# Attention with a soft mixture of experts: the last weights by column halves for two experts in place of three, the first output by halves for eighteen tokens a row in place of fifteen

## The chip, the cores and the metric

The kernel runs on one core of a Trainium2 chip. The metric is the device time of one execution in microseconds (us), the median of several. Beside it there is one profiled execution, with its own time and its span: the span runs from the first to the last instruction of the trace, the time also covers what lies around them.

## The reference

Sliding-window attention (8 batches, 8 heads, 576 positions, head size 64, window 64) makes the 4608 x 512 matrix x. A soft mixture of 8 experts with 4 slots each follows:

```python
def _moe_ref(x, phi, w1, w2):
    logits = x @ phi                                  # 4608 x 32
    d = softmax of logits over the tokens
    slot_input = (d.T @ x).reshape(8, 4, 512)
    for e in range(8):
        h = np.maximum(slot_input[e] @ w1[e], 0.0)    # 512 -> 1024
        slot_out[e] = h @ w2[e]                       # 1024 -> 512
    c = softmax of logits over the slots
    return c @ slot_out                               # 4608 x 512
```

Inputs and output are 32-bit floats. The slots' input needs the softmax over all tokens, so the experts come after the whole attention; the output needs the slots' result of all experts, so no row of it can be written before the last expert's weights are in.

## The kernel before

**Attention.** 32 steps (pairs of heads) run through a pipeline written out by hand: transposes of k and q, row maxima, scores, exponentials, products with v, and in between the logits, the running softmax over the tokens and the sum for the slots' input. q, k, v and the weights are loaded by GpSimd, whose transfers turn 32-bit floats into 16-bit ones on the way. All of these loads stand in one queue, in the order in which GpSimd issues them. There are eight semaphores for them, used in turn, so an issue waits until the transfer eight places before it has landed; what stands behind it on GpSimd waits too.

**Weights.** `w1_t[e]` and `w2_t[e]` hold the first and second matrices of the experts. Those of experts 0 to 6 have room of their own. `load_w(i)` (L136) loads a whole one, 1 MB in 16 bit: i = 0 to 6 are first matrices, i = 7 to 13 second ones, so that i = 12 is the second matrix of expert 5. In the loop over the steps twelve of them are issued (i = 0 to 11). Expert 7's matrices take over buffers of the staged k and q: `load_last1` (L146) loads a quarter of its first matrix, `load_half` (L154) a piece of its second.

`load_half(i)` loads a quarter of the second matrix of an expert, 256 KB: rows of one half (h) and columns of one half (d). Before the change it counts through experts 5, 6 and 7, first for the left 256 columns (i = 0 to 5), then for the right ones (i = 6 to 11). Eight of these are issued at L733, when the last staged rows have gone, the other four in the expert phase, between the `cb_sub` (L532), which GpSimd also computes.

**Experts.** `first` (L859) and `turn_hidden` (L874) make the hidden values, all experts of a group of four at once, in parts of the array. `second_first` (L881) multiplies with the second matrices of experts 0 to 3, over all columns. `second(d)` (L887) does it for experts 4 and 5 in column half d, `second_last(d)` (L893) for experts 6 and 7. Sums are gathered in `ops[d]`; a copy by ScalarE turns that into `osb`, the right side of the last product, each column half by itself (L967, L979).

**Output.** A row of the output is taken from the softmax over the slots: `ct4[k]` holds it, transposed, for 1152 tokens (k = 0 to 3), nine per partition, made by `spread` (two batches each); `sums(k)` makes the reciprocals of its sums. `give(k, e0, ne, c0, nc_)` (L940) computes `ne` of the nine tokens of each partition, from column c0 on, `nc_` columns wide: a matmul per token into `cp`, an eviction that scales it by the reciprocal, by turns on ScalarE (L957) and VectorE (L955), and one transfer to memory by SyncE (L959). A piece of ne tokens has, for each partition, ne runs of 1 KB if it is half the columns wide, and one run of ne x 2 KB if it is whole, since the nine tokens of a partition follow one another in memory. The pieces take seven buffers in turn (`obs`, the place of first matrices that are no longer used), so that an eviction of a piece waits for the transfer seven pieces before it.

The engines' queues run in the order of the program text: on TensorE `second(0)`, `second_last(0)`, left halves of k = 0, `second(1)`, left halves of k = 1, `second_last(1)`, right halves, and the rest with both halves together.

Of the kernel before, what the change touches and what calls it, by code (L numbers as in the profile page):

```python
# [18 lines left out]
def kernel(  # L19
# [12 lines left out]
    B, H, S, Dh = q.shape  # L32
# [97 lines left out]
    def w1_dram(e):  # L130
        return moe_w1[e].rearrange("(p c) f -> p c f", c=NKK)

    def w2_dram(e):
        return moe_w2[e].rearrange("(h p c) d -> p h c d", h=2, c=NFC // 2)

    def load_w(i):  # L136
        second, e = divmod(i, NRES)
        if second:
            nc.gpsimd.dma_start(out=w2_t[e, 0][:, :, :].rearrange("p (h c) d -> p h c d", h=2), in_=w2_dram(e))
        else:  # L140
            nc.gpsimd.dma_start(out=w1_t[e, 0], in_=w1_dram(e))

    last = E - 1
# [8 lines left out]
    DH = D // 2  # L152

    def load_half(i):  # L154
        d, i = divmod(i, 6)
        e, h = last - 2 + i // 2, i % 2
        if e == last:
            if h == 0:
                w2_t[last].append([])
            c = pin.tile([128, 4, DH], FP16, name="w2h", tag="ks")  # L160
            w2_t[last][d].extend(c[:, j, :] for j in range(4))
        else:
            c = w2_t[e, 0][:, 4 * h:4 * h + 4, DH * d:DH * d + DH]
        nc.gpsimd.dma_start(out=c, in_=w2_dram(e)[:, h, :, DH * d:DH * d + DH])

    def w2_at(e, d, fc):
        return w2_t[e][d][fc] if e == last else w2_t[e][fc][:, DH * d:DH * d + DH]
# [362 lines left out]
    def cb_sub(b, eng):  # L530
        lgT = lgs[b]
        eng.tensor_tensor(out=lgT[:, :, :], in0=lgT[:, :, :],  # L532
                          in1=cbs[b][:, :].unsqueeze(2).broadcast_to([128, 6, 32]), op=ALU.subtract)
# [7 lines left out]
    def cb_turn(b):  # L541
        nc.vector.transpose(ct_all[:, b, :], cbs.pop(b)[:, :, :].rearrange("p i s -> p (i s)"))
# [144 lines left out]
    NE = 2 * S // 128  # L687
# [12 lines left out]
    def spread(b, copy, rp=None):  # L700
        if rp is None:
            rp = psr.tile([128, 1024], FP32, name="rp", tag="rp")
        for t in range(5):
            w = 128 if t < 4 else 64
            nc.tensor.matmul(rp[:, 128 * t:128 * t + w], ss4[:, min(t, 3), :],
                             ct_all[:, b, 128 * (t // 4):128 * (t // 4) + w], start=True, stop=True,
                             skip_group_check=True)
        copy(out=ct4[b // 2][:, :, 64 * (b % 2):64 * (b % 2) + 64],
             in_=rp[:, 0:S].rearrange("p (x e) -> p e x", e=NE))
# [7 lines left out]
    def sums(k):  # L717
        rp = psr.tile([128, 1024], FP32, name="rp", tag="rp")
        for e in range(NE):
            nc.tensor.matmul(rp[:, e:e + 1], ct4[k][:, e, :], one[:, :], start=True, stop=True, skip_group_check=True)  # L720
        nc.vector.reciprocal(rcs[:, k, :], rp[:, 0:NE])  # L721
# [8 lines left out]
    load_last1()  # L730
    make_ss4()
    nc.gpsimd.tensor_copy(out=ssf, in_=ss)
    for i in range(8):  # L733
        load_half(i)
    st_score8(p - 3)
    st_exp8(p - 3)
# [122 lines left out]
    def first(g, f2):  # L859
        ha, _ = bank("ha")  # L860
        for kk in range(NKK):
            for j in range(4):
                nc.tensor.matmul(ha[32 * j:32 * j + 32, :], sit[:, kk, :],
                                 w1_t[4 * g + j][kk][:, 512 * f2:512 * f2 + 512],
                                 start=(kk == 0), stop=(kk == NKK - 1), skip_group_check=True)

        hv = ha[:, :].rearrange("p (x c) -> p c x", c=4)
        if f2 == 0:
            nc.scalar.activation(hs_[:, g, f2], hv, AF.Relu, scale=emask[:, g:g + 1])
        else:  # L870
            nc.vector.tensor_scalar(out=hs_[:, g, f2], in0=hv, scalar1=emask[:, g:g + 1],
                                    scalar2=0.0, op0=ALU.mult, op1=ALU.max)
# [21 lines left out]
    def second_last(d):  # L894
        for j in (2, 3):
            for fc in range(NFC):
                i = fc % 4
                nc.tensor.matmul(ops[d][32 * i:32 * i + 32, :], hT[1][:, fc, 32 * j:32 * j + 32],
                                 w2_at(4 + j, d, fc), start=False, stop=(j == 3 and fc >= 4), skip_group_check=True)
# [3 lines left out]
    fr_turn(b)  # L903
    cb_max(b - 2)
    cb_sub(b - 2, nc.gpsimd)
    load_half(8)
    cb_turn(b - 3)
    first(0, 1)
    spread(1, act)
    cb_max(b - 1)  # L910
    cb_sub(b - 1, nc.gpsimd)
    load_half(9)
    first(1, 0)
    turn_hidden(0)
    sums(0)
    cb_exp(b - 2)
    cb_max(b)
    cb_sub(b, nc.gpsimd)
    load_half(10)
    load_half(11)  # L920
    first(1, 1)
    second_first(range(4))
    turn_hidden(1)
# [16 lines left out]
    def give(k, e0, ne, c0, nc_):  # L940
        nonlocal turn, piece
        ov = out[2 * S * k:2 * S * k + 2 * S, :].rearrange("(p e) d -> p e d", e=NE)
        ob = obs[piece % NRES][:, 0:ne * nc_].rearrange("p (e d) -> p e d", d=nc_)
        piece += 1
        n1 = 512 // nc_
        for i0 in range(0, ne, n1):
            n_ = min(n1, ne - i0)
            cp = pst.tile([128, n1, nc_], FP32, name="cp", tag="cp")
            for i in range(n_):
                nc.tensor.matmul(cp[:, i, :], ct4[k][:, e0 + i0 + i, :], osb[:, c0:c0 + nc_],  # L950
                                 start=True, stop=True, skip_group_check=True)
            for i in range(n_):
                rc = rcs[:, k, e0 + i0 + i:e0 + i0 + i + 1]
                if turn % 2:
                    nc.vector.tensor_scalar(out=ob[:, i0 + i, :], in0=cp[:, i, :], scalar1=rc, scalar2=None, op0=ALU.mult)  # L955
                else:
                    nc.scalar.activation(ob[:, i0 + i, :], cp[:, i, :], AF.Copy, scale=rc)  # L957
            turn += 1
        nc.sync.dma_start(out=ov[:, e0:e0 + ne, c0:c0 + nc_], in_=ob)  # L959
# [15 lines left out]
    sums(1)  # L975
    give(1, 0, 3, 0, DH)
    give(1, 3, 3, 0, DH)
    second_last(1)
    act(out=osb[:, DH:D], in_=ops[1])  # L979
    give(0, 0, 2, DH, DH)  # L980
# [3 lines left out]
    give(1, 0, 3, DH, DH)  # L984
    spread(5, dve)
    give(1, 3, 3, DH, DH)
    for k in range(1, B // 2):
        for e0 in range(6 if k == 1 else 0, NE, 3):
            give(k, e0, 3, 0, D)
            if k == 1:  # L990
                sums(2)
            if k == 2:
                if e0 < 6:
                    spread(6 + e0 // 3, (act, dve)[turn % 2])
                else:
                    sums(3)
# [28 lines left out]
```

## Time and profile before

| what | us or share |
|---|---|
| median of 3 executions | 192.83 (192.33 to 192.84) |
| the profiled execution, its time | 192.84 |
| its span | 191.1 |
| TensorE busy (matmuls) | 159.7 (84%) |
| VectorE busy | 143.6 (75%) |
| ScalarE busy | 129.6 (68%) |
| GpSimd busy | 108.2 (57%) |
| bytes moved by the DMA engines | 41.46 MB, 9.44 MB of it output |
| first and last output transfer issued | 158.6 and 181.9 |

The page gives, besides, a strip of 40 slices for each engine, with the DMA engines' busy share in tenths and the bytes moved, the chain of work that ended last, and the issues of transfers with their sizes. The trace has, for each transfer, its issue and its landing, and for each of the sixteen DMA engines the moment at which that engine's part has landed. Transfers of the loads are counted with their 16-bit bytes; twice as many are read from memory.

### The profile page before, as it was taken

How to read it: one execution, taken by the hardware profiler on the slowest of the kernel's cores; microseconds unless marked ns; L12 is line 12 of the kernel's file. 1: busy time of each engine (PE TensorE's matmuls, PEld its weight loads, DVE VectorE, ACT ScalarE, POOL GpSimd, SP SyncE). 2: the span in 40 equal slices, each digit the busy share in tenths (PEclk: the TensorE clock that was granted, in tenths of full speed). 3: DMA queues.
4: the chain of work that ended last, by engine and by line, in shares of the span. 5: the costliest groups of instructions: out<-in, count | busy, mean ns of one | idle time of the engine just before them, and what ended most of it. 6: DMA issues, size and time to landing. Idle time of an engine off the chain costs nothing. (4 is left out here: it accounts for less than half of the span.)

```text
span 191.1 us, 6805 instructions
## 1 busy us (share of the span) xinstructions
PE 159.7 (84%) x2887; PEld 115.8 (61%) x2887; DVE 143.6 (75%) x354; ACT 129.6 (68%) x249; POOL 108.2 (57%) x181
## 2 busy tenths in 40 slices
PE   7976989989999999998999999889889967189700
PEld 2555878876876877787687687757634544054200
DVE  5888788888888898899889889889864618058900
ACT  5576787887787787789788778875863525068700
POOL 7956876966869487598668748540935830000000
PEclk9999999999999999999999999999999999658975
DMA  6999999999999999999999999999999999959996
GB/s 164 216 188 182 187 189 219 175 222 180 185 225 177 219 182 185 224 178 215 188 186 213 187 206 196 212 203 205 212 209 200 198 194 234 292 196 356 408 417 253
DMA packets 64798, 41.46 MB, mean 217 GB/s; under 512 B 38912, under 2 KB 61184, under 8 KB 63872
## 3 DMA queue, kind: packets, MB, share of 16 engines
q0 software_dynamic: 58400, 30.35, 116.4%
q1 hardware_dynamic: 6368, 10.68, 16.0%
q8 instruction: 22, 0.36, 0.7%
q14 instruction: 8, 0.07, 0.1%
HBM read 61.93 MB, written 9.44 MB: 374 GB/s over the span
## 5 line engine op out<-in xcount | busy, mean ns | idle before, releaser
L391 DVE TENSOR_REDUCE m<-a_m 128x8 f16<-128x1024 f32 x32 | 39.1, 1220 | 0.0
L425 ACT ACTIVATE pt<-a_s 128x1024 f16<-128x1024 f32 x32 | 32.8, 1024 | 7.8 <-PE a_s L418 7.6
L359 POOL COPY qb<-qp 64x288 int32<-64x288 int32 x54 | 22.8, 423 | 23.3 <-ACT qp L356 19.9
L477 ACT COPY xt<-a_k 128x576 f16<-128x576 f16 x28 | 17.9, 638 | 12.7 <-PE a_k L473 12.7
L459 DVE TENSOR_TENSOR x_b<-a_v,rc 128x640 f16<-128x640 f32 x31 | 25.6, 824 | 1.1
L955 DVE TENSOR_SCALAR w<-cp,rcs 128x256 f32<-128x256 f32 (+1 forms) x25 | 13.5, 585 | 12.0 <-PE cp L950 11.3
L351 ACT ACTIVATE kT<-a_k 128x576 f16<-128x576 f16 x31 | 20.3, 655 | 1.0 <-PE a_k L340 1.0
L405 DVE TENSOR_TENSOR rt<-a_v,kind 36x256 f16<-36x256 f32 x30 | 12.8, 428 | 9.9 <-PE a_v L404 9.3
L180 POOL DMA_DIRECT2D v<-in_v_dram x16 | 20.1, 1254 | 0.0
L386 PE MATMUL a_m<-kT,qb 128*128 128x128 f16 x256 | 19.8, 220 | 0.0
L412 PEld LDWEIGHTS <-kT 128*128 128x128 f16 x288 | 18.6, 98 | 1.8 <-issue 1.4
L412 PE MATMUL a_s<-qb,kT 128*128 128x128 f16 x256 | 19.6, 219 | 0.0
L418 PE MATMUL a_s<-rt,lh 128*128 128x256 f16 x128 | 19.2, 273 | 0.4 <-DVE rt L405 0.4
L356 ACT ACTIVATE qp<-a_q 128x576 f16<-128x576 f16 x27 | 18.0, 668 | 1.7 <-PE a_q L340 1.7
L386 PEld LDWEIGHTS <-qb 128*128 128x128 f16 x256 | 14.6, 98 | 7.3 <-issue 5.4
L190 POOL COPY v<-v 64x576 int32<-64x576 int32 x16 | 10.6, 662 | 14.1 <-DMA v<-in_v_dram 13.6
L340 PE MATMUL a_q<-ident_h,qs 96*64 96x96 f16 x384 | 15.2, 207 | 2.8 <-DVE a_q L237 1.5
L449 PE MATMUL a_v<-v,pt 128*64 128x65 f16 x558 | 15.1, 195 | 0.6 <-DVE rt L405 0.4
L957 ACT ACTIVATE w<-cp,rcs 128x256 f32<-128x256 f32 (+1 forms) x26 | 12.7, 564 | 4.1 <-PE cp L950 2.5
L340 PEld LDWEIGHTS <-qs 96*64 96x64 f16 x384 | 12.5, 110 | 4.7 <-issue 4.4
L340 PE MATMUL a_k<-ident_h,ks 96*64 96x96 f16 x384 | 14.5, 212 | 0.1
L950 PE MATMUL cp<-qb,v 128*128 128x256 f16 (+1 forms) x51 | 12.7, 368 | 2.1 <-ACT w L957 1.1
(194 smaller groups left out, 351.0 us busy)
## 6 DMA issues: line engine op xcount, KB each, us to landing
w<-in_moe_w_dram POOLq DMA_DIRECT2D x12, 1024.0 KB, 15.9
out_dram<-w SPq DMA_DIRECT2D x7, 768.0 KB, 5.8
v<-in_v_dram POOLq DMA_DIRECT2D x16, 288.0 KB, 12.8
ks<-in_k_dram POOLq DMA_DIRECT2D x15, 288.0 KB, 13.6
qs<-in_q_dram POOLq DMA_DIRECT2D x15, 288.0 KB, 12.2
w<-in_moe_w_dram POOLq DMA_DIRECT2D x8, 256.0 KB, 10.4
out_dram<-w SPq DMA_DIRECT2D x5, 384.0 KB, 3.3
w1h<-in_moe_w_dram POOLq DMA_DIRECT2D x4, 256.0 KB, 16.3
```

The lines of the kernel that those rows point to most:

```text
L180: nc.gpsimd.dma_start(out=v1s[b % 2][:, c, 0:Dh], in_=v[b].rearrange("h s d -> (h s) d").rearrange("(c p) d -> p c d", p=128)[:, c, :])
L340: nc.tensor.transpose(tq[64 * hf:64 * hf + 64, RP * r:RP * r + RP], src[0:RP, h + hf, Dh * r:Dh * r + Dh], ident_h[0:RP, 0:RP])
L351: nc.scalar.activation(kTs[p % NK][:, 64:64 + S], turned(a_kh), AF.Copy, scale=QKS)
L356: nc.scalar.activation(qp, turned(a_qh), AF.Copy, scale=QKS)
L359: nc.gpsimd.tensor_copy(out=qbs[p % NQ][:, :, :, :].rearrange("p i l x -> p (i l x)").bitcast(mybir.dt.int32) .rearrange("p (i l x) -> p i ...
L386: nc.tensor.matmul(a_m[:, i // 4, 128 * (i % 4):128 * (i % 4) + 128], qblock(p, i), kwindow(p, i), start=False, stop=True, skip_group_chec ...
L391: nc.vector.reduce_max(m.rearrange("p e j -> p j e"), a_m[:, :, :].rearrange("p l (j e x) -> p (l j) e x", e=2, x=128), axis=AXX)
L412: nc.tensor.matmul(at(i), kwindow(p, i), qblock(p, i), start=(i % 4 == 0), stop=False, skip_group_check=True)
L418: nc.tensor.matmul(a_s[:, i // 4, 128 * (i % 4):128 * (i % 4) + 256], lh[:, i // 2, :], rt[:, :], start=False, stop=True, skip_group_check ...
L425: nc.scalar.activation(st_pt(p)[:, 0:8, :].rearrange("p i x -> p (i x)"), a_s[:, :, :], AF.Exp, scale=XS)
L459: nc.vector.tensor_tensor(out=xbs[b][:, :, 128 * hp:128 * hp + 128].rearrange("p c (l d) -> p l c d", l=2), in0=avv[:, :, :, 0:64], in1=rc ...
L477: nc.scalar.copy(out=xts[b][:, hp, :], in_=th[:, 0:S])
```

## The change

- `load_half` counts through two experts, 6 and 7, instead of three: eight pieces in all instead of twelve. The second matrix of expert 5 is loaded whole by `load_w(12)`, ahead of them.
- Five pieces are issued at L733 instead of eight, and three in the expert phase instead of four.
- The last three tokens of k = 1 are written by halves as well: `give(1, 6, 3, 0, DH)` after the other left halves, `give(1, 6, 3, DH, DH)` after the other right ones, so that all eighteen tokens per partition of k = 0 and 1 go out by halves, in twelve pieces. The piece of three whole rows of k = 1 goes; the whole rows begin with k = 2.
- `sums(2)`, which stood behind that piece, now stands before the last right half.

```diff
     def load_half(i):
-        d, i = divmod(i, 6)
-        e, h = last - 2 + i // 2, i % 2
+        d, i = divmod(i, 4)
+        e, h = last - 1 + i // 2, i % 2
...
-    for i in range(8):
+    load_w(12)
+    for i in range(5):
         load_half(i)
...
     cb_sub(b - 2, nc.gpsimd)
-    load_half(8)
+    load_half(5)
...
     cb_sub(b - 1, nc.gpsimd)
-    load_half(9)
+    load_half(6)
...
     cb_sub(b, nc.gpsimd)
-    load_half(10)
-    load_half(11)
+    load_half(7)
...
     give(1, 0, 3, 0, DH)
     give(1, 3, 3, 0, DH)
+    give(1, 6, 3, 0, DH)
     second_last(1)
     act(out=osb[:, DH:D], in_=ops[1])
...
     give(1, 3, 3, DH, DH)
-    for k in range(1, B // 2):
-        for e0 in range(6 if k == 1 else 0, NE, 3):
+    sums(2)
+    give(1, 6, 3, DH, DH)
+    for k in range(2, B // 2):
+        for e0 in range(0, NE, 3):
             give(k, e0, 3, 0, D)
-            if k == 1:
-                sums(2)
             if k == 2:
```

## The prediction

> **What bounds the kernel now.** I read the page first: its strips of the span in 40 slices (row 2) and the chain that ended last (row 4).
>
> ```profile
> DMA  6999999999999999999999999999999999959996
> GB/s 164 216 188 182 187 189 219 175 222 180 185 225 177 219 182 185 224 178 215 188 186 213 187 206 196 212 203 205 212 209 200 198 194 234 292 196 356 408 417 253
> ...
> ACT 1%; PE 1%; ACTq 0%; DVE 0%; issue 0%
> ```
>
> The chain covers under 3% of the span: after the last evictions, at about 181.8 us, no engine computes, and 9 us pass in which only transfers run. The DMA strip stands at 9 from the second slice on, with one slice of 5 (167 to 172 us). So the DMA engines set the end, and that one slice is the place where they could do more. Next, the DMA view of 165 to 171 us (each digit 0.15 us), then the instructions of the tail in order of time (start, length, engine, line; in brackets the idle time before and what ended it):
>
> ```profile
> DMA  9999766666565555443434343422100001899999
> ```
>
> ```profile
> 156.55 0.29 PE L898 MATMUL op<-w2h,hT 128*32 128x256 f16 x4 [1.10 <-DMA w2h<-in_moe_w_dram]
> 158.64 24.40 SPq L959 DMA_DIRECT2D out_dram<-w  x17
> 163.78 0.40 PE L898 MATMUL op<-w2h,hT 128*32 128x256 f16 x4 [1.58 <-DMA w2h<-in_moe_w_dram]
> 166.78 0.40 PE L898 MATMUL op<-w2h,hT 128*32 128x256 f16 x4 [2.60 <-DMA w2h<-in_moe_w_dram]
> ```
>
> The first column half of the slots' result ("left half") is complete when its last weights land, 156.5; its fifteen rows (a row is one token on each of 128 partitions) start moving at 159.9. The right half's last weights land only at 166.7, and its rows start at 170.06. By then the left half has run out, hence the hole. The strip falls as a slope from 165.5 to 169.7, not as a step: the sixteen DMA engines are not level. The trace's landing records (one event per engine and transfer) give the reason: each engine has a fixed sixteenth of every transfer and works through its own list. The transfer that ends the weights of w1 (last of four, issued 135.2) is done on the first engine at 144.17, on the sixth at 144.87, on the last four at 148.05 to 148.43, and this lag of 4.3 us stays to the end of the left half (165.60 on the first, 170.08 on the last). After the hole all start level: the last piece lands between 189.54 and 189.76, on one engine at 190.01. **The end is therefore set by the last engine's list, not by the mean of sixteen.** I make the sum on that engine.
>
> **Durations** (DMA views of stretches with one kind of packet: packets, MB moved, mean rate; loads are counted in fp16 bytes):
>
> ```profile
> DMA packets 138, 0.54 MB, mean 215 GB/s; under 512 B 8, under 2 KB 8, under 8 KB 137
> ```
> ```profile
> DMA packets 2735, 1.37 MB, mean 196 GB/s; under 512 B 82, under 2 KB 2734, under 8 KB 2734
> ```
> ```profile
> DMA packets 701, 0.69 MB, mean 343 GB/s; under 512 B 32, under 2 KB 701, under 8 KB 701
> ```
> ```profile
> DMA packets 825, 4.57 MB, mean 415 GB/s; under 512 B 82, under 2 KB 82, under 8 KB 824
> ```
>
> These are 136 to 138.5 us (whole weight matrices, 4 KB packets), 152 to 159 (column halves, 512 B), 173.5 to 175.5 (output by halves, 1 KB) and 178 to 189 (whole output rows, 6 KB). Per transfer, from the landing records: a 256 KB column half every 1.335 us on each engine; a whole 1 MB matrix (L139, issued 124.65) 4.89 us after its predecessor on most engines, 5.17 on the last; a piece of three whole rows 1.90; three half rows 1.12 to 1.18, four 1.60, so 0.38 for one (0.365 by the view above, 0.40 at most).
>
> **The change, part by part, on the last engine.**
>
> 1. *Loads.* Four half transfers of expert 5 go and one whole one comes, at the head of the list: 4.89 - 4 x 1.335 = -0.45 us (at worst 5.17, -0.17). Bytes are the same. On GpSimd four issues of 0.74 us become one of about 0.70 (L139's row). An issue waits for the transfer eight places before it, as now (3.5 us at 143.7). The whole one, issued at 138, lands at 148.4 + 4.9 = 153.3, and the last half, eight places behind it, is issued then (now 154.07), with seven transfers, over 9 us of work, still in the queue; the queue does not run dry. The three cb_sub (0.52 each) keep their order; five halves instead of eight issue ahead of the first, so they come earlier if anything. Cost nothing, covered by the full queue; without that cover a late issue would cost its 0.7 us.
>
> 2. *Left half later.* Ahead of its last weights now lie 1 MB + 4 halves: 148.43 + 4.89 + 4 x 1.335 = 158.66 in place of 156.51, 2.15 later. With the same 3.4 us from there to the first output packet, output starts at 162.03. This costs nothing on the last engine, which loads until 158.66 + 4 x 1.335 = 164.0 anyway. It does cost the first engines, which are through with weights at 159.7 and idle 2.3 us; but they lead by 4.3. If the cover fails (engines level), those 2.3 us are the price.
>
> 3. *Three more rows by halves.* Six half rows in place of one piece of three whole rows: 6 x 0.38 - 1.90 = +0.38 us (0.29 to 0.50). Evictions: six of 0.42 (L957, L955) in place of three of 0.6 to 0.7, on engines that wait for DMA anyway; hidden behind pieces in flight.
>
> 4. *The hole.* The last engine now ends the left half at 170.08 and lands the next piece (two half rows, 0.76) at 171.39: 0.55 idle, and 0.07 more is lost at 172 us, where the second transfer of four rows took 1.59 in place of 1.52. After the change it has weights to 164.0, then eighteen rows of 0.38: to 170.8. The right half's weights land at 164.0 to 166 (see the rivals), its first packets follow 3.3 us after: 167.3 to 169.3, before 170.8. So the wait is gone: -0.62 (-0.4 at least, by the idle to the first packet, 170.06, plus its start). What waits next is nothing on this engine; on the first ones, whose left half ends at 162.03 + 6.84 = 168.9, at most 0.4.
>
> 5. *Moved sums(2).* Nine matmuls (0.37) and a reciprocal (0.21) run after six pieces instead of seven; behind them on TensorE stands the last piece of k = 1. Hidden by 1.1 us of DMA per piece; 0.6 if not. Weights and output overlap on the last engine for 2 us in place of 4.5, a gain now of 0.1 (170.18 by sum, 170.08 measured) shrinks: +0.05.
>
> Sum: -0.45 + 0.38 - 0.62 + 0.05 = -0.64. Check along the list: 164.0 + 36 x 0.38 + 6 x 1.90 = 189.1, and about 0.3 by which this engine falls behind its fellows at 178 (178.71 against 178.3): 189.4 against 190.01. From the profiled execution's 192.84 (span 191.1, 1.7 around it; the median, 192.83, is the same): **192.2 us**.
>
> A rule against the row: the Trainium skill (DMA: Bandwidth & Descriptors, Specifications) gives 512 B as the smallest transfer at line rate. By it a half row would cost half of a whole one, step 3 would be nothing, and the sum 191.8. The trace disagrees: 343 GB/s at 1 KB, 415 at 6 KB.
>
> **Rivals.**
>
> *Bad ends of the prices* (0.18): the whole load takes 5.17, a half row 0.40, the idle gives 0.4: -0.17 + 0.50 - 0.40 = -0.07, **192.75**. For it: 5.17 is this engine's own number. Against: its extra 0.28 looks like an instruction fetch, not the load.
>
> *The hole moves with the left half* (0.07; slower). Once output starts, it shares each engine with the remaining weights, and the last weight transfer took 3.0 us on the last engine in place of 1.335. If they are starved further, so that the right half lands 10.2 us after the left as now (156.5 to 166.7), it lands at 168.9 and its packets start at 172.2: 172.2 + 18 x 0.38 + 11.4 + 0.3 = 190.7, **193.6**. It decides once the right half lands after 167.5 (170.8 - 3.3). Against: at 162.03 only 2.0 us of weights are left on the last engine (4.5 now); at half share they take 4, to 166.0. The Trainium skill (same page, Queues, rings and completion order) says an engine takes its queues in turn, packet by packet: this half share. The 3.0 against 1.335 agrees.
>
> *A lag step on a late engine* (0.11; slower). One engine lost 1.2 us within one transfer (153.50 to 154.70 at its landing, where its neighbours moved on by 1.33) and joined the late ones; instruction fetches (the page's queues q8 and q14) are the likely cause. On one of the last four it costs all of it: 192.2 + 1.2 = **193.4**. For it: the order of loads changes, so fetches fall elsewhere. Against: there were few such steps.
>
> *Engines level out* (0.08). If late engines catch up while the first idle, the end follows the mean: output from 162.03 with 0.4 of weights left, 162.4 + 13.7 + 11.4 = 187.5, some 2 below 189.6: **190.9**. Against: the lag held for 20 us.
>
> **Numbers.** Forecast 0.56, its own range 191.7 to 192.6. 0.3% is 0.58 us, about what can be told from no change: faster is below 192.25, slower above 193.4. The forecast lies near that edge; about 0.36 of its 0.56 counts as faster, with the level engines 0.44. Same: its other 0.20, the bad ends and a little of the lag step, which lies on the bound, 0.40. Slower: the moved hole and the rest of the lag step, 0.16. The range, 191.2 to 193.3, leaves out the level engines and the moved hole, 0.15.
>
> **What would show it.** Right: left half's last L898 wait ends near 158.7, first output issue near 160.8, right half's wait ends between 164 and 166.5, the strip has no slice of 5 there but a dip near 160 to 162, and a sloped end of up to 2 us at 187 to 189.5. Wrong: a hole after 168, or a level end.

## The result

The changed kernel takes 190.79 us (median of six, 190.41 to 191.36), the kernel before 192.26 beside it (192.13 to 192.84): a ratio of 0.9917, 95% interval 0.9895 to 0.994, or 1.5 us. The forecast was 192.2, a gain of 0.64, with a range from 191.2: the direction was right, the gain more than twice as large, and the time lies below the range. The six executions of the kernel before include the three that the forecast started from (median 192.83); the other three took 192.13 to 192.20, so 0.57 of the 1.4 us between 192.2 and 190.79 lies in the base and not in the gain. The profiled execution took 190.96 us with a span of 189.2. Of all executions in this document one is far from its fellows and left out of the figures: the profiled one of `e11`, 244.18 us at a granted clock of 0.57.

The DMA strip and the bytes moved, on the page of the changed kernel:

```profile
DMA  6999999999999999999999999999999999999996
GB/s 165 216 185 184 187 183 225 176 222 181 185 223 181 212 188 185 215 187 210 195 182 212 192 198 199 208 211 192 218 210 211 209 195 180 258 353 344 406 417 265
```

No slice is below 9 any more between the second and the last but one. The DMA view of 165 to 171 us, and the one of 162 to 168 below it (0.15 us a digit), of the changed kernel:

```profile
DMA  9999999999999999999999999999999999999999
```
```profile
DMA  9999999996438999999999999999999999999999
```

The hole of before is gone. What is left of idle time is a dip of 0.6 us at 163.5, and the gap in front, where the first engines have no weights left and output has not begun; in the view of 158 to 164 us it shows as the 7s and 8s before the first output packet at 161.92 (162.03 had been worked out):

```profile
DMA  9999999999999999988878876699999999995449
```

The tail in order of time:

```profile
158.60 0.40 PE L899 MATMUL op<-w2h,hT 128*32 128x256 f16 x4 [1.05 <-DMA w2h<-in_moe_w_dram]
161.00 19.87 SPq L959 DMA_DIRECT2D out_dram<-w  x18
164.77 0.39 PE L899 MATMUL op<-w2h,hT 128*32 128x256 f16 x8
165.21 0.37 ACT L980 CAST qb<-op 128x256 f16<-128x256 f32 x1
```

The left half's last wait for weights ends at 158.6 and its first piece is issued at 161.0 (forecast 158.7 and 160.8). For the right half TensorE does not wait at all: the last eight matmuls stand without a wait, as its weights, landed at 163.92, were there before it came to them. The copy to `osb` comes at 165.2, 2 us earlier than before, although output began 2 us later.

**Where the extra gain is.** The landing records give sixteen times for each piece, without the engines' names; the last time of each piece is taken for the last engine's. In the profiled execution of the changed kernel it stands 0.8 us or more behind the one before it until 174.0, so that up to there it is surely one engine:

```
last engine, changed kernel       from      to        us     forecast
end of its weights                          163.92           164.0
first four half rows              163.92    166.25     2.33   1.52
thirty-two half rows              166.25    177.06    10.81  12.16   (0.338 each, 0.38 taken)
six pieces of three whole rows    177.06    188.20    11.14  11.40   (1.857 each, 1.90 taken)
falling behind at 178                                  0      0.3
```

At the median of the sixteen engines the thirty-two rows took 0.396 each, the idle time of the dip included, and the whole pieces 1.899. From the third piece on, behind the dip, a half row took 0.384 at the median and 0.340 on the last engine. So the last engine was faster than the others, and its lag behind the median fell from 2.39 us to 0.52 by the end of the half rows and 0.27 at the end.

### The profile page after: what moved, and what is told of

Its sections match the earlier page's. It is cut to its first block, busy times and chain, and to the rows that moved or that the text cites. A ratio compares the mean times of both kernels' runs of the same rounds, so it can differ in the third digit from the quotient of the medians.

```text
span 189.2 us, 6815 instructions
## 1 busy us (share of the span) xinstructions
PE 158.2 (84%) x2890; PEld 114.9 (61%) x2890; DVE 143.8 (76%) x356; ACT 129.6 (69%) x250; POOL 105.9 (56%) x178
## 4 chain that ended last, share of the span: by engine, by line
PE 35%; DVE 31%; DMA 20%; issue 4%; ACT 3%; POOL 1%; DVEq 0%; SPq 0%; ACTq 0%
DMA w1h<-in_moe_w_dram 10%; DVE m L391 9%; DMA w2h<-in_moe_w_dram 7%; DVE x_b L459 5%; PE a_m L386 5%; DVE rt L405 3%; PE a_q L340 3%; PE a_s L412 3%; PE a_m L382 3%; PE a_s L418 3%; PE a_k L340 3%; PE cp L950 3%; DVE m L401 2%; DMA w<-in_q_dram 2%; PE a_v L397 2%
## 5 line engine op out<-in xcount | busy, mean ns | idle before, releaser
L449 PEld LDWEIGHTS <-pt 128*64 128x64 f16 x576 | 13.2, 111 | 1.1 <-issue 0.4
```

The lines of the kernel that those rows point to most:

```text
L449: nc.tensor.matmul(a_v[r0:r0 + 64, hf, 65 * (i // 2):65 * (i // 2) + 65], pt[:, i, 64 * hf:64 * hf + 64], rhs, start=True, stop=True, skip ...
```

## The experiments

Theory L is the one on record: each engine keeps its lag, the last one's list sets the end, and it works at the pace that all have when they are in step. The first rival (M) was that engines level out and the total of all counts. After the first four runs (`e1` to `e4`) a narrower form took its place (N): an engine that lags works faster than those in step, those that land their pieces at the same moment.

### Which part of the change gains: the loads or the output

`e1_loads_only` takes the change's loads and the output of before:

```diff
-    give(1, 6, 3, 0, DH)
...
-    sums(2)
-    give(1, 6, 3, DH, DH)
-    for k in range(2, B // 2):
-        for e0 in range(0, NE, 3):
+    for k in range(1, B // 2):
+        for e0 in range(6 if k == 1 else 0, NE, 3):
             give(k, e0, 3, 0, D)
+            if k == 1:
+                sums(2)
```

> The loads of the change (expert 5 whole, experts 6 and 7 by halves), but the output of before: fifteen rows by halves, the last three tokens of k = 1 whole. Theory L (as predicted: each DMA engine keeps its lag, the last engine's list sets the end, a half row costs 0.38 us on it): -0.45 for the loads, -0.62 for the hole, +0.05, so 1.0 us below the kernel before and 0.4 below the changed one, if the changed one behaved by this theory. Theory M (engines that lag behind the others catch up while the output is written, so that the end follows the total of all sixteen): the idle of the first engines counts as well, 1.5 to 2.2 us below the kernel before, and since three whole rows are moved faster than six half rows (1.9 against 2.3 us) 0 to 0.4 below the changed one. Under both the left half's last weights land near 158.6 us and no slice falls to half.

Measured: 190.29 us, 0.988 of the kernel before (0.9856 to 0.9903), 2.3 us less than its 192.65. In a second measurement, side by side with the changed kernel:

> The changed kernel itself, once more, beside the next three on the same chip: 0.990 to 0.993 of the kernel before.

> e1_loads_only once more, in the same rounds as the changed kernel; the two differ by six half rows in place of one piece of three whole rows. Theory N (half row 0.34 us on an engine that lags, 0.387 on one in step; three whole rows 1.85 or 1.905): 0.2 to 0.4 us below the changed kernel. If it is 0.7 or more below, as the two separate measurements have it, the extra rows cost more than their transfers, and the start of the output or the lag at the weights' end must differ too.

The changed kernel 0.991 (0.9892 to 0.9928), e1 0.9902 (0.9877 to 0.9927), both 190.87 us, less apart than the 0.2 to 0.4 worked out. So the loads alone bring the gain, and the three additional rows by halves bring nothing on top of it; what they cost is too small for these runs.

`e2_output_only` is the reverse: `load_half` and its calls as before, the output of the change.

> The loads of before (experts 5, 6 and 7 by halves), with the output of the change: eighteen rows by halves. Left half ready at 156.5 us as before, first output near 159.9. Theory L: the last engine's idle (0.55 to 0.62) goes, six half rows for three whole ones cost 0.38: 0.2 us below the kernel before, between 0 and 0.4. Theory M: of the 2.5 us that an engine idles on the mean between the halves, 1.1 are filled, 0.38 are paid: 0.6 to 0.8 below. A hole near 168 to 170 us stays under both, shorter by 1.1 us than before.

Measured: 191.62 us, 0.9952 (0.9936 to 0.9968), 0.9 us below; L's bound was 0.4, M's 0.8. The hole is shorter and still there, in the DMA view of 158 to 171 us (0.33 us a digit):

```profile
DMA  9999999999999999999999999887666644438999
```

Its last engine took 0.366 for a half row and 1.824 for a whole piece, against 0.401 (the hole included) and 1.935 (a loss of 0.3 us at 178 included) in the kernel before.

### How many rows by halves

`e3_twelve_rows` has the change's loads and four left pieces, where the changed kernel has six and the kernel before has five:

```diff
     give(1, 0, 3, 0, DH)
-    give(1, 3, 3, 0, DH)
-    give(1, 6, 3, 0, DH)
...
-    give(1, 3, 3, DH, DH)
-    sums(2)
-    give(1, 6, 3, DH, DH)
-    for k in range(2, B // 2):
-        for e0 in range(0, NE, 3):
+    for k in range(1, B // 2):
+        for e0 in range(3 if k == 1 else 0, NE, 3):
             give(k, e0, 3, 0, D)
+            if k == 1 and e0 == 3:
+                sums(2)
```

> The loads of the change, and only twelve rows by halves: the last six tokens of k = 1 are written whole. Theory L: the last engine has its left half done at 164.0 + 12 x 0.38 = 168.5 us, the right half's first packets come near 167.8, so it never waits: 0.76 us less than the changed kernel. Theory M: the first engines end their left half at 162.3 + 4.6 = 166.9 and wait 0.9 us; of the 0.76 saved 0.3 to 0.5 are given back: 0.3 to 0.5 less than the changed kernel. If the right half comes later than 168.6, a hole opens again and it is slower than the changed kernel.

Measured: 190.64 us, 0.9903 (0.9879 to 0.9928), not distinguishable from the changed kernel, where the theories had it 0.3 to 0.8 us lower. The same view as above shows a hole at 166.5 with twelve rows, in which the engines at the front idle:

```profile
DMA  9999999987899997999999999639999999999999
```

### Order or size of the loads

`e5_order_only` is e1 with expert 5 in four half pieces at the head:

```diff
-    load_w(12)
+    for d in range(2):
+        for h in range(2):
+            nc.gpsimd.dma_start(out=w2_t[5, 0][:, 4 * h:4 * h + 4, DH * d:DH * d + DH],
+                                in_=w2_dram(5)[:, h, :, DH * d:DH * d + DH])
     for i in range(5):
         load_half(i)
```

> As e1_loads_only, but expert 5's second matrix comes as four column-half pieces at the head of the list (both left ones, both right ones) in place of one whole transfer: only the order of the loads of before is changed. If the order is what gains (the right half 5.3 us behind the left in place of 10.2, so no hole) and the whole transfer only its 0.45 us, this is 0.45 us above e1_loads_only, some 1.8 us below the kernel before. If the whole transfer is the greater part (fewer, larger packets, shorter lags between the engines), it falls back to within 0.8 us of the kernel before.

Measured: 190.86 us, 0.992 (0.9888 to 0.9951), 1.7 us below. The order alone, with the same twelve pieces as before, is most of the gain; against e1 (0.988 and 0.9902) the whole transfer is worth 0.3 to 0.8 us by the medians, with intervals that overlap, so nothing is possible too.

`e6_one_expert` goes further the same way: experts 5 and 6 whole, 7 by halves, nine rows by halves.

```diff
     def load_half(i):
-        d, i = divmod(i, 4)
-        e, h = last - 1 + i // 2, i % 2
+        d, h = divmod(i, 2)
+        e = last
...
     load_w(12)
-    for i in range(5):
+    load_w(13)
+    for i in range(1):
         load_half(i)
```

> One step further: experts 5 and 6 whole, expert 7 alone by halves, and nine rows by halves (k = 0 only). Left half ready near 160.9 us, first output near 164.2, 2 us after e1_loads_only; the right half 2.7 us behind the left. Every engine is through with its weights before output starts, so all idle and start level. From there 18 half rows of 0.38 and nine whole pieces of 1.88: 164.2 + 6.8 + 16.9 = 188 against 186.9 in e1_loads_only: 0.8 to 1.3 us above e1_loads_only. If small pieces cost more than their rows show (0.7 us for six half rows in the changed kernel against e1_loads_only, where 0.38 was expected), it is level with it.

Measured: 193.05 us, 1.003 (1.0012 to 1.0047): 0.5 us slower than the kernel before, and 2.2 to 2.8 above e1, where 0.8 to 1.3 had been worked out. The strip of 158 to 171 us has the front gap, down to nothing from 162.5 to 163.5, and at 165.2 and 167.4 two short holes:

```profile
DMA  9999998888754100079998099999900799999999
```

The right half's weights landed at 162.9, but its first piece was issued at 167.3: the left half's pieces, `second(1)` and `sums(1)` stand ahead of it on TensorE, whose granted clock was 0.71 from 160 to 167 us. With so short a distance between the halves it is computing that comes late. No run takes the half clock away here, so what share of the wait is the clock's stays open.

`e8_two_and_a_half` lies between before and change:

```diff
-        d, i = divmod(i, 4)
-        e, h = last - 1 + i // 2, i % 2
+        d, i = divmod(i, 5)
+        e, h = last - 2 + (i + 1) // 2, (i + 1) % 2
...
-    load_w(12)
-    for i in range(5):
+    nc.gpsimd.dma_start(out=w2_t[5, 0][:, 0:4, :], in_=w2_dram(5)[:, 0, :, :])
+    for i in range(6):
         load_half(i)
```

> Between before and change: of expert 5 the first half of the rows comes whole, the second half by column halves; eighteen rows by halves as in the changed kernel. Left half ready 1.3 us earlier than in the changed kernel (157.3), first output near 160.8, the weights' end 0.2 later, so more of them share the engines with output; right half ready 164.5 to 166, its first packets 168 to 169.3, where the first engines end their left half (160.8 + 6.8 = 167.6). If the start of output decides, 0.5 to 1 us below the changed kernel; if the total on the last engine's list decides, it is level with it (0.2 above); a hole at 168 of up to 1.5 us on the first engines would show in the strip.

Measured: 190.31 us, 0.9882 (0.9864 to 0.99). Again with the changed kernel, together with the same loads and fifteen rows (`e9`, which is e8 with the output of e1):

> e8_two_and_a_half once more in the same rounds: 0.3 to 0.7 us below the changed kernel and level, within 0.4, with e1_again.

> The loads of e8 with fifteen rows by halves as in e1. Six half rows fewer and three whole ones more save 0.2 us on a lagging engine and 0.4 on one in step, as in e1_again; but the first engines end their left half at 160.5 + 15 x 0.387 = 166.3 to 167 and the right half's first packets come near 168.3, so they wait over 1 us, while the last engine (left half done near 169.3 in e8, 168.2 here) hardly waits. Theory N, by which the last engine's list and its pace set the end: level with e8_again, between 0.3 below and 0.2 above. If the idle of the first engines counts as much as the last one's, it is 0.4 to 0.8 above e8_again.

Measured: e8 190.35 us, 0.9886 (0.9864 to 0.9908); e9 190.40 us, 0.9875 (0.9857 to 0.9893); the changed kernel beside them 0.991. The two are level, as the last engine's list has it, though the first engines of e9 have a dip at 166.6. Both are 0.2 to 0.4% below the changed kernel; the intervals overlap.

### Does a lagging engine keep its lag

`e7_one_engine_late` puts one engine behind by force. The transfer reads 127 rows of w1 to a place that nobody reads any more.

```diff
     spread_product(3)
+    nc.sync.dma_start(out=ct_all[0:127, 0:4, :].rearrange("p b s -> p (b s)").bitcast(FP32)[:, 0:256],
+                      in_=moe_w1[0][0:127, 0:256])
```

> The changed kernel with one more transfer on SyncE's queue ahead of the first output piece: 127 rows of 1 KB of w1, read to a place that nobody reads (computes nothing; 127 rows are not divisible by sixteen, so that one engine should carry all of them). That engine then stands some 5 to 6 us behind the others. Theory L (a lagging engine works at the pace of the others, 0.38 for a half row, 1.90 for three whole ones): it stays behind by all of it, and the end comes 4 to 6 us later than the changed kernel's, all landings of one engine late by the same amount. Theory N (a lagging engine is faster than those in step: 0.335 for a half row, 1.83 to 1.86 for three whole ones, as the last engine showed in the changed kernel): it makes up 36 x 0.045 + 6 x 0.05 = 1.9 us, and the end comes 2 to 4 us later. If the lag goes wholly (the engines share one limit and the late one takes what the others leave), the end comes under 1 us later.

Measured: 192.00 us, 0.9972 (0.9956 to 0.9987), some 1.1 us above the changed kernel, less than the 2 to 4 of theory N. One engine alone is late in the landing records (first engine, median, last; the late one is the last):

```
piece landed                           first    median    last    last behind median
second (after 4 half rows)            163.41    163.97   168.25    4.28
third (after 9)                       166.17    166.3    169.88    3.6
twelfth (after all 36)                176.54    176.67   179.10    2.4
eighteenth (after 6 whole pieces)     187.94    188.04   190.16    2.1
```

From the third to the twelfth piece the late engine took 9.22 us for 27 half rows, 0.341 each, the first engine 10.37, 0.384. Whole pieces took it 1.843, the first 1.90. The end of the strip shows it alone at work for 2 us, in the view of 186 to 191.1 us of this run (0.13 us a digit), against the changed kernel's from 186 to 189.2 (0.08 us a digit):

```profile
DMA  9798989599891201010101101010100000000000
```
```profile
DMA  9599599799799599775020000000000000000000
```

Theory L needed 0.384 for the late engine; it falls. Both paces were taken at nearly the same time, so the number of engines at work does not explain them. N holds in kind and in the size of the two paces; its time was missed, as the lag was 4.3 us at the second piece and not 5 to 6. The other profiles agree: from the second piece on the last engine took 0.337 to 0.358 for a half row in the changed kernel (0.338, 0.350), e1 (0.358, 0.339), e3 (0.337), e5 (0.346), e8 (0.341, 0.341) and e9 (0.340), while the first engine took 0.396 to 0.42 with its idle time in dips and holes; in the changed kernel, from the third piece on, it took 0.383. The lag did not go wholly, so that one late engine still costs something.

`e4_two_queues` asked whether those at the head are held back by the queue that feeds them:

```diff
-        nc.sync.dma_start(out=ov[:, e0:e0 + ne, c0:c0 + nc_], in_=ob)
+        (nc.sync, nc.gpsimd)[piece % 2].dma_start(out=ov[:, e0:e0 + ne, c0:c0 + nc_], in_=ob)
```

> The changed kernel, with every other output piece issued by GpSimd (idle by then) in place of SyncE, so that two queues feed the DMA engines with output. In the changed kernel the last engine, 1.2 us behind, takes 0.34 us for a half row, the others 0.38. If the others are held back by how fast one queue hands out its pieces (they are at its head, the last engine has a backlog), they go at 0.34 too with two queues: 18 rows x 0.04 to 36 x 0.04, 0.7 to 1.4 us less than the changed kernel. If it is the engines or the memory that take 0.38 when all work in step, the time stays within 0.4 us of the changed kernel's, or is worse by GpSimd's own issue time.

Measured: 191.93 us, 0.9961 (0.9948 to 0.9974), about 0.9 us worse than the changed kernel. Bytes moved from 167.6 to 171.8 us, in this run and then in the changed kernel:

```profile
DMA packets 925, 1.37 MB, mean 327 GB/s; under 512 B 64, under 2 KB 765, under 8 KB 925
```
```profile
DMA packets 1502, 1.47 MB, mean 350 GB/s; under 512 B 65, under 2 KB 1502, under 8 KB 1502
```

Two queues did not make the half rows faster: on the first engine three of them took 1.16 us each time (pieces landed at 167.41, 168.57 and 169.73), 0.387 for one. So a slow queue as the cause is not supported. It brought gaps of its own (GpSimd issues later), so it does not exclude it for good.

### TensorE's clock while it waits

The traces show the granted clock at one half from 163.4 to 173.6 us in the kernel before, and from 158.6 to 162.0 in the changed one. The windows of the kernel before from 155 us on (stretch and length, busy time of TensorE, its weight loads, VectorE, ScalarE and GpSimd, then the clock, the DMA share, GB/s):

```profile
155.00:162.30 7.30, 4.73 (x61) 2.98 (x61) 4.19 (x10) 3.27 (x9) 0.00 (x0) 1.00 1.41 219
162.30:167.00 4.70, 0.62 (x8) 0.22 (x7) 0.00 (x0) 0.00 (x0) 0.00 (x0) 0.61 0.97 296
167.00:170.50 3.50, 2.74 (x19) 1.88 (x16) 1.55 (x4) 1.94 (x5) 0.00 (x0) 0.50 0.40 136
170.50:174.00 3.50, 3.41 (x26) 1.98 (x25) 2.61 (x6) 2.84 (x7) 0.00 (x0) 0.56 1.00 331
```

The waits for the right half's weights left TensorE little to do, and the right half's first pieces ran at half clock. The Trainium skill (TensorE: Matmul & The Clock Gate, Part 1) puts the step down to a half after one idle window of some 3.4 us. Here it came without one: in the 3.4 us before it fell TensorE was busy for 1.46 us in the kernel before, and for 0.59 in the changed one, in groups of four matmuls with waits of about 1.05 us between them. Three versions fill the waits of `second_last` with matmuls that nobody reads, into a spare bank:

```diff
     def second_last(d, fills):
         for j in (2, 3):
             for fc in range(NFC):
                 i = fc % 4
+                if i == 0:
+                    fill(fills[2 * (j - 2) + fc // 4], spare)
...
+    pfl = ctx.enter_context(tc.tile_pool(name="pfl", bufs=1, space=bass.MemoryType.PSUM))
+    spare = pfl.tile([128, 512], FP32, name="spare")[:, :]
```

> The kernel before, with matmuls that nobody reads in the waits of second_last(0) (four) and second_last(1) (sixteen, in waits of 0.8, 1.6 and 2.6 us). The clock should stay at 1 between 163 and 174 us. The right half's first piece is issued 2.4 us after its last weights at half clock; at full clock that is some 0.4 to 0.8 less (osb to first piece 1.95 us, of it 1.65 for seven matmuls that take about 0.9 at full clock). The hole shortens by as much on every engine: 0.4 to 0.8 us below the kernel before, if the last engine, which idled 0.55, is taken with it; 0 to 0.2 if not. The change's gain over a kernel with its clock up would then be that much less.

> The changed kernel with nine matmuls (three in each of the last three waits of second_last(0), some 0.21 us each, into a spare bank that nobody reads), so that TensorE does not stand idle while it waits for the left half's weights. The granted clock should stay at 1 from 158 to 165 us, the nine matmuls of the first pieces take 1.03 us in place of 2.08, the first output packets come 0.3 to 0.6 us earlier. If the last engine's list sets the end (it loads until 164 anyway), the time is that of the changed kernel within 0.3. If the start of output for all engines sets it, 0.4 to 0.7 us less.

> The same filling (eight matmuls) in e9, the version with two and a half experts by halves and fifteen rows: clock at 1 from 157 on, first output 0.3 to 0.5 us earlier; 0 to 0.4 us below e9 (0.9875 of the kernel before), so 0.985 to 0.988.

Measured: the kernel before, filled, 191.21 us, 0.994 (0.9924 to 0.9955), 1.2 us less, more than either expectation; the changed kernel, filled, 190.10 us, 0.9874 (0.9859 to 0.9888), against 0.991 and 0.9917 unfilled; e9, filled, 190.03 us (median of five), 0.9883 (0.9863 to 0.9903), no change. In the first two the clock stayed at 1, shown here for the kernel before, filled; for the third no trace shows it:

```profile
162.30:167.00 4.70, 4.22 (x29) 2.02 (x28) 0.47 (x2) 0.43 (x2) 0.00 (x0) 1.00 0.98 311
167.00:170.50 3.50, 2.36 (x23) 1.53 (x21) 3.21 (x8) 3.47 (x9) 0.00 (x0) 1.00 0.79 268
```

How far the clock is the cause can't be told from these, since something else moved with it. In each trace of the kernel before and of the changed one, filled or not, a 16 KB instruction transfer (the page's queue q8, one packet, about 0.95 us) runs at some 162 to 163 us. In both profiles of the changed kernel the last engine alone took 0.5 to 0.7 us more for its first two half rows than its late neighbours (1.70 and 1.57 us against at most 1.02), in the filled one it did not (0.99 against 1.01). The records do not say which engine carried the instruction transfer, so that it is the reason is argued only. In the kernel before the last weights landed at 166.74, in the filled one at 165.01, and the first right piece was issued 2.4 us and 2.6 us after them: in the profiles the gain is in the landing, not in the computing behind it. The last weight transfer took 3.0 to 3.1 us there on each of the last four engines and 2.2 to 2.4 in the filled kernel, which one instruction transfer on one engine does not explain; why it is faster stays open. So the pace of TensorE, the effect looked for, is not shown to matter there.

The two traces of e1, the same kernel, differ in the clock too (first 189.69 us, then 191.34):

```profile
160.00:162.00 2.00, 1.77 (x30) 1.28 (x30) 2.00 (x5) 1.27 (x4) 0.00 (x0) 1.00 1.02 184
160.00:162.00 2.00, 2.00 (x12) 1.13 (x12) 1.03 (x3) 1.40 (x4) 0.00 (x0) 0.50 0.84 113
```

Of the 1.7 us between them 0.9 was there when the last weights landed (163.44 and 164.36). Behind that, the last engine's first four half rows took 1.42 and 2.30 us, and the rest was no longer at the slower clock than at the faster (21.85 and 22.01). In the ten executions of e1, the six with a mean granted clock of 0.967 or more took 189.69 to 190.60 us, the four of 0.963 or less 190.79 to 191.55. So the clock and the time go together; which brings which, these runs do not show.

## Why the prediction was wrong in size

**The bound was right.** DMA sets the end, the hole between the halves is what the change removes, and the removal comes from the loads: e5, e1.

**Step 1** (the whole transfer, -0.45): right in the trace, where the whole matrix landed on the last engine 4.89 us after its predecessor (148.31 to 153.20), as taken; in the times of e5 and e1 it can be anything from nothing to 0.8.

**Step 2** (left half 2.15 later, at no cost on the last engine): right. Left half's weights at 158.56 (158.66), first output packet at 161.92 (162.03), end of weights at 163.92 (164.0).

**Step 3** (three more rows by halves, +0.38): too small to be measured; 0.991 against 0.9902 side by side, and 0.9886 against 0.9875 for e8 and e9. At 0.34 a half row, six of them cost 0.2 more than a whole piece of 1.86. **Step 5** (+0.05) is separated by no run.

**Step 4** (the hole, -0.62): right in kind; the wait between the halves is gone on every engine.

**The step that failed is the price of a half row on the last engine, "0.38 for one", and of a whole piece, 1.90.** Both came from 170 to 189 us of the kernel before, where the hole had just put all sixteen engines in step. After the change nothing makes the last engine level with the others, it stays behind, and behind it is faster: 0.338 and 1.857. Over 32 rows and six pieces this is 1.35 + 0.26 us, and the 0.3 of falling behind did not come; the first four rows lost 0.8, beside an instruction transfer at 163.2. With 0.08 for the earlier end of the weights, the list was 1.2 us too long: 189.4 worked out, 188.20 measured. The right rows stood in the trace of before: its last engine landed pieces of three half rows, late and out of step, at 168.05, 169.08 and 170.08, 0.34 a row, and from 180.88 to 190.01, 0.7 to 0.4 us behind the median, it took 1.83 for a whole piece. Step 5 had read the half rows as a gain from sharing with the weights; and as the first engines had no more to write from 165.6 on, that row alone could not tell an engine that lags from one that has fewer beside it. e7 shows the effect by itself.

**The rivals.** "Engines level out" (0.08, 190.9) gave the time that came, and the lag did fall to 0.3 us; its argument against, that the lag had held for 20 us, was about loads. Loads do hold it (half pieces land every 1.335 us on early and late engines alike), output doesn't. That its time came is partly luck: one engine 4.3 us late kept 2.1 of it to the end in e7, so the end does not follow the mean. "A lag step on a late engine" (0.11) did occur, in both profiles of the changed kernel, and cost 0.7 to 0.8; it was hidden by the rest. "The hole moves with the left half" (0.07) did not: the last weights landed at 163.92, before the 167.5 from which it would decide. There the Trainium skill (DMA: Bandwidth & Descriptors, Queues, rings and completion order) has an engine take its queues in turn, by packets; on the last engine the last weight transfers landed 1.32 and 1.36 us after those before them although output had been issued since 161.0, so no half share is seen there. In the kernel before, 3.0 us for the last one agrees with it.

**What was to show it wrong.** "A level end" had been named, and it came: the last piece lands between 187.78 and 188.20, where a slope of up to 2 us had been forecast.

**What stays open.** Why an engine out of step writes 12% faster is not settled; two queues did not change the pace of those in step. No run separates lagging from merely being apart: in the kernel before the first engine, ahead of its neighbours by 0.1 to 0.2 us, took 1.11 us for three half rows (landed at 163.38, 164.49 and 165.60), 0.37 for one, between the two paces, though there others were still loading. Nor is it known how the 0.7 us of the filled changed kernel divide between the clock and the instruction transfer.

## What to carry to other kernels

Where transfers set the end, make the sum on the last engine's list, but take each price from rows in which that engine is as far out of step as it will be; a price from a stage where all engines started together is too high. Put loads that a first output needs, and those that the second needs, so close that output never waits for the second: here the order alone was worth 1.7 us, one step further lost it again to computing.

## What the runs showed of the hardware that was not expected

- An engine that lags behind the others writes faster than they do: 0.341 against 0.384 us for its 8 KB of a half row, 1.843 against 1.90 for a piece of whole rows (e7). In loads no such difference was seen: seven half pieces took 9.36 us on the first engine and on the last (changed kernel, 150.37 to 159.73 and 154.56 to 163.92).
- An instruction transfer of 16 KB, one packet of about 0.95 us, runs at much the same place in each program (queue q8, at 161.9 to 164.5 us in sixteen traces). Beside it the last engine of the changed kernel lost 0.5 to 0.7 us; that it was this engine that carried the transfer is not shown.
- TensorE's granted clock fell to one half after 3.4 us with 0.59 us of matmuls in them, in waits of about 1 us (changed kernel), and after 3.4 us with 1.46 in them (kernel before).
